# Sixteen 32x32 tiles for the last stage of the kernels' transform, and another memory order for its two results

## The chip, the cores and the metric

The kernel runs on one core of one Trainium2 chip. The metric is the device time of one execution in microseconds (us): the median of three runs, beside the lowest and the highest. The profile is of a further execution, which has its own time and its own span (first to last instruction).

The engines are called as in the profile: PE (TensorE's matmuls) and PEld (its weight loads), DVE (VectorE), ACT (ScalarE), POOL (GpSimd), SP (SyncE, whose queue starts most DMAs). PSUM is the matmuls' result memory, here eight banks of 128 partitions x 512 f32.

## What is computed

Four layers on a sequence of 2048 rows of 640 channels: attention, a state-space layer, attention, the same state-space layer.

```python
x = x + A(layernorm(x))      # attention, 32 heads of 20 channels, projection wo
x = x + B(layernorm(x))      # state-space layer
x = x + A(layernorm(x))
x = x + B(layernorm(x))

# B: a convolution as long as the sequence, one kernel per channel, by FFT
P = exp((A * dt)[:, :, None] * pos)
K = 2.0 * einsum("dn,dnl->dl", C, P).real       # 640 kernels of 2048 values
y = irfft(rfft(u, 4096) * rfft(K, 4096), 4096)[:, :, :2048]
return y + u * D_skip
```

The kernels K are the same in both B layers, so their transform is computed once.

## The kernel before, in words

**The stages in order of time.** First attention, beside which a generator `kgen` computes K and stores it in DRAM (`kd`). Then the first output projection (`out_proj`, lines 1130 to 1150), beside which the kernels' transform (`ktransform`, lines 1056 to 1125) runs. Then the first state-space layer (`ssm`, lines 1165 to 1303). Then attention, output projection and `ssm` once more, without `kgen` and without the transform.

**The output projection** handles 16 row tiles `s`. For each it loads a 128 x 640 piece of the attention's result (`otl`), splits it into two parts (`oh` on ACT, `ol` on DVE), runs 30 matmuls of 128 x 320 into two PSUM tiles of the pool M, adds them to `x`, and after every second `s` makes the normalised rows `uh` and `ul` that `ssm` reads (ACT, then POOL). `ssm` can begin when all sixteen are there.

**The kernels' transform** handles five blocks of 128 channels (`unit_load(b)`):
1. Load 1 MB, `kl` (128 channels x 2048), two buffers, the next block's load started at the block's begin; add the skip value to the first column.
2. 16 transposes in four groups into PSUM tiles `pkt` (pool T, two banks); ACT writes `ktrh`, DVE the remainder `ktrl`, both f16.
3. Eight PSUM tiles `pkx` (pool X, two banks), 12 f16 matmuls each; ACT or DVE copies each into `x1` (profile name `kx`).
4. A loop over eight quarters `q` of 4 x 128 columns: four transposes of `x1` into `pkt` (pool T); ACT scales them into `xt` (`kxt`); one f32 matmul with the 128 x 128 matrix `f2` into `pkf` (pool F, two banks; the profile shows it as two instructions of 128 x 512); two shuffles on DVE, which write the result's real half twice into `kn0` and its imaginary half twice into `kn1`; a multiplication of `kn1` by a sign per partition, on ACT. After two quarters `kn0` and `kn1` (512 KB each) are stored into the DRAM tensors `kha` and `khb`.

**In `ssm`** each of 40 steps loads a quarter of a block of both tensors, `ka` and `kb` (256 KB each, three buffers each), multiplies by `ka` on DVE (`t1`), by `kb` on POOL (line 1226) and adds on POOL (line 1227).

**What sets the order.** Each engine works through its own list in order. The lists are made when the program is built: of the instructions whose inputs and buffers are free by then, the one that the code emitted first goes first. `out_proj` emits the whole transform in the middle of its third row tile (`weave(1000)`), so the transform goes first and the later row tiles fill the time in which it waits. A buffer pool that is opened over the memory of earlier pools waits for the last use of those. During attention most orders are tied by hand (`chain`); in the transform and in `out_proj` none are.

Of the kernel before, what the change touches and what calls it, by code (L numbers as in the profile page):

```python
# [21 lines left out]
P = 128  # L22
L = 2048
# [61 lines left out]
def mha_s4d_kernel(ctx, tc, x_in, wqkv, wo, lar, aim, cr, ci, ldt, dsk,  # L85
                   c_e1, c_eb, c_f2, c_fa, c_sel, c_lv, c_id, c_sg, c_e16, c_f16, c_id16, out, parts="asas", general=None):
# [28 lines left out]
    kha = dram.tile([P, D // 4, P], F32, name="kha")  # L115
    khb = dram.tile([P, D // 4, P], F32, name="khb")
# [933 lines left out]
    DUP0 = list(range(16)) * 2  # L1050
    DUP1 = list(range(16, 32)) * 2

# [3 lines left out]
    def ktransform(e1):  # L1056
# [4 lines left out]
        f2 = c1.tile([P, P], F32, name="f2")  # L1061
        sy.dma_start(f2, c_f2)
        sgn = c1.tile([P, 1], F32, name="sgn")
        sy.dma_start(sgn, c_sg)

        skip = c1.tile([P, NCT], F32, name="skip")
        sy.dma_start(skip, dsk)

        def load(b):
            kl = c2.tile([P, L], F32, name="kl")  # L1070
            sy.dma_start(kl, kd[b * P:b * P + P, :])
            return kl
        kls = [load(0)]

        def unit_load(b):
            kl = kls.pop()
            if b + 1 < NCT:
                kls.append(load(b + 1))
# [11 lines left out]
            x1 = c1.tile([P, 32, NI // 2, 16], F32, name="kx1")  # L1090
            for i2 in range(NI // 2):
                ps = pst("X", [P, 2, 2, P], F32, tag="X", name="pkx")
                for i in range(2):
                    s = 2 * i2 + i
                    for r in range(2):
                        for n, (e, m) in enumerate(((0, hi), (0, lo), (1, hi))):
                            te.matmul(ps[:, r, i, :], e1[:, e, s, r, :], m[:, s, :], start=(n == 0), stop=(n == 2))
                (ve.tensor_copy if i2 % 4 == 1 else se.copy)(by_channel(x1, i2), ps.rearrange("p r i (g c) -> p (r i) g c", c=4))
                yield
            prev = None  # L1100
            for q in range(9):
                if q < 8:
                    pt = pst("T", [P, 4, P], F32, tag="T", name="pkt")
                    for g in range(4):
                        te.transpose(pt[:, g, :], x1[:, 4 * q + g].rearrange("p i s -> p (i s)"), ident)
                    xt = c2.tile([P, 512], F32, name="kxt")
                    se.activation(xt, pt.rearrange("p g k -> p (g k)"), AF.Copy, scale=ksc[:, 1:2])
                if prev is not None:
                    g0 = b * 32 + 4 * (q - 1)
                    if q % 2:  # L1110
                        kn = [c2.tile([P, 2, 512], F32, name=f"kn{s}") for s in range(2)]
                    px = pst("F", [P, 512], F32, tag="F", name="pkf")
                    te.matmul(px, f2, prev, start=True, stop=True)  # L1113
# [49 lines left out]
    def ssm(x, uh, ul, consts, last):  # L1163
# [19 lines left out]
        with ExitStack() as c:  # L1183
# [29 lines left out]
            def stage2b(b, q, xt):  # L1213
# [3 lines left out]
                sy.dma_start(ka, kha[:, g0:g0 + 4, :].rearrange("p g k -> p (g k)"))  # L1217
                sy.dma_start(kb, khb[:, g0:g0 + 4, :].rearrange("p g k -> p (g k)"))
# [217 lines left out]
def _constants():  # L1436
# [13 lines left out]
    for s, o, m in ((0, 0, C), (1, 0, S), (0, 1, -S), (1, 1, C)):  # L1450
        fa[:, s, :, :, o] = np.einsum("hli,cd->hlcid", m.reshape(4, 4, 16), e4)
    f2 = f2.reshape(2, NI // 2, 2, 4, P).transpose(1, 0, 2, 3, 4)
    sg = np.zeros((4, 2, 16, 1))
    sg[:, 0], sg[:, 1] = -1.0, 1.0
# [5 lines left out]
    cs = dict(c_e1=e1.reshape(P, -1), c_eb=eb.reshape(P, -1), c_f2=f2.reshape(P, P), c_sg=sg.reshape(P, 1),  # L1460
              c_fa=fa.reshape(P, -1), c_sel=sel.reshape(P, -1), c_lv=lv, c_id=np.eye(P))
    cs = {n: np.ascontiguousarray(a.astype(np.float32)) for n, a in cs.items()}
    for n, a in (("c_e16", e1), ("c_f16", f2)):
# [9 lines left out]
          "c_e1", "c_eb", "c_f2", "c_fa", "c_sel", "c_lv", "c_id", "c_sg",  # L1473
# [31 lines left out]
```

## Time and profile before

| | us |
|---|---|
| time, median of 3 runs | 2690.48 |
| lowest to highest | 2688.76 to 2694.98 |
| the profiled execution, time | 2693.68 |
| its span | 2691.8 |
| first attention, first S matmul to last row | 113.3 to about 1102 |
| first output projection, its matmuls | 1102.3 to about 1273 |
| transform, first to last matmul | 1132.8 to 1246.9 |
| first `ssm`, first matmul | 1272.9 |

The granted clock of TensorE was 0.996 over the span. A row of a group reads: line, engine, operation, written tile <- read tiles, shape and type, count; then busy time, mean ns of one. Line 77 is the helper through which ACT, DVE, POOL and SP operations of the ordered engines go, so these are told apart by their tiles. A matmul's duration has its way through the array in it: the time from one start to the next is shorter. In rows by stretch the columns are the stretch, its length, the busy time of each engine (with its number of instructions), then the granted clock, the mean busy share of the 16 DMA engines, and GB/s.

### The profile page before, as it was taken

To read this page: it belongs to the slowest core of one execution; us is meant where nothing else is said; L and a number is where in the kernel's file an instruction comes from. 1 tells how busy PE (TensorE), PEld (TensorE's weight loads), DVE (VectorE), ACT (ScalarE), POOL (GpSimd) and SP (SyncE) were. 2 spreads that over 40 slices of the span, in tenths; PEclk is the share of its full clock that TensorE was granted. 3 is DMA by queue.
4 is the path that set the end of the run, shared out by engine and by line. 5 is a ranking of instruction groups with operands and counts; after the bars stand their busy time and mean duration, and the time that the engine had idled before them with its cause. 6 is when DMAs were issued, how large, how long until landed. Compare 5 with 4: busy or idle time off the path is not lost.

```text
span 2691.8 us, 116010 instructions
## 1 busy us (share of the span) xinstructions
PE 2519.0 (94%) x51104; PEld 1432.0 (53%) x51104; DVE 1473.7 (55%) x3295; ACT 2364.3 (88%) x2799; POOL 855.2 (32%) x1283
## 2 busy tenths in 40 slices
PE   7899999999999998899998999999999998888998
PEld 3345444444444443678886444454444443335888
DVE  8687877876856993477776332232232221003865
ACT  7899999999999999676655899999999999996464
POOL 1123323333332334301671122222222223222476
PEclk9999999999999999999999999999999999999999
DMA  6513222322221225354542111111121112112365
GB/s 212 177 49 88 64 77 53 88 58 72 62 54 50 56 66 169 109 229 161 185 146 65 49 52 52 52 56 42 47 63 39 52 39 59 41 37 80 115 189 162
DMA packets 183154, 236.48 MB, mean 88 GB/s; under 512 B 42864, under 2 KB 128368, under 8 KB 180976
## 3 DMA queue, kind: packets, MB, share of 16 engines
q1 hardware_dynamic: 146304, 182.38, 21.2%
q0 software_dynamic: 36336, 46.59, 7.4%
q8 instruction: 403, 6.60, 1.0%
q14 instruction: 111, 0.91, 0.1%
HBM read 152.81 MB, written 76.03 MB: 85 GB/s over the span
## 4 chain that ended last, share of the span: by engine, by line
ACT 50%; PE 27%; issue 9%; DVE 6%; DMA 3%; SPq 1%; POOL 0%; ACTq 0%; DVEq 0%; POOLq 0%
ACT pt L77 49%; PE pa L862 4%; PE psv L1233 3%; PE psy L1243 3%; PE S L845 3%; PE po L1139 2%; PE psx L1221 2%; PE m L598 2%; PE psx L1198 1%; PE po L1133 1%; PE pkf L1113 1%; PE pst L1208 1%; DVE ktab L77 1%; DMA qop<-qs 1%; PE pq L751 1%
## 5 line engine op out<-in xcount | busy, mean ns | idle before, releaser
L77 ACT ACTIVATE pt<-S 128x1024 f32<-128x1024 f32 x2048 | 1921.9, 1037 | 37.5 <-PE S L845 28.4
L862 PE MATMUL pa<-pt,V 64*32 64x512 f32 x16384 | 1102.2, 590 | 1.7 <-DVE oc L77 1.2
L845 PE MATMUL S<-qop,kop 61*32 61x512 f16 x16384 | 883.6, 381 | 114.4 <-ACT pt L77 102.6
L845 PEld LDWEIGHTS <-kop 61*32 61x32 f16 x16384 | 374.0, 89 | 772.3 <-issue 651.4
L862 PEld LDWEIGHTS pa<-pt,V 64*32 64x32 f32 x16384 | 316.9, 106 | 73.4 <-issue 9.1
L77 POOL DMA_DIRECT2D dn<-oc x256 | 126.2, 499 | 709.3 <-DVE oc L77 682.4
L77 DVE TENSOR_SCALAR qc<-m 128x512 f32<-128x512 f32 (+1 forms) x68 | 46.8, 689 | 305.0 <-PE m L598 302.4
L77 DVE COPY oc<-pa 128x512 f32<-128x512 f32 x64 | 44.2, 690 | 305.1 <-PE pa L862 297.4
L77 POOL DMA_DIRECT2D db<-dn x256 | 129.5, 511 | 129.7 <-DMA dn<-dr 126.4
L598 PE MATMUL m<-xh,wh 64*32 64x512 f16 x2560 | 147.9, 379 | 5.0 <-DVE qc L77 5.0
L598 PE MATMUL m<-xh,wl 64*32 64x512 f16 x2560 | 148.7, 377 | 0.0
L598 PE MATMUL m<-xl,wh 64*32 64x512 f16 x2560 | 146.6, 377 | 0.0
L598 PEld LDWEIGHTS <-wh 64*32 64x32 f16 x5120 | 92.8, 93 | 78.0 <-issue 35.7
L77 POOL DMA_DIRECT2D ot<-oc x256 | 130.3, 516 | 3.1 <-DVE oc L77 1.7
L1226 POOL TENSOR_TENSOR t<-t,kb 128x512 f32<-128x512 f32 x80 | 101.9, 1275 | 67.8 <-DVE t L77 66.8
L77 ACT COPY xt<-pst 128x1024 f16<-128x1024 f16 x80 | 81.6, 1023 | 46.7 <-PE pst L1208 46.6
L77 POOL DMA_DIRECT2D dn<-dr x64 | 35.8, 560 | 245.3 <-DVE dr L77 235.5
L77 DVE TENSOR_TENSOR kb<-ktab 128x512 f32<-128x512 f32 x160 | 107.7, 692 | 0.0
L77 DVE TENSOR_SCALAR V<-m 128x160 f32<-128x160 f32 x64 | 20.7, 324 | 157.7 <-PE m L564 157.7
L564 PEld LDWEIGHTS <-xh 128*128 128x128 f16 x960 | 79.7, 98 | 47.0 <-issue 31.6
L1227 POOL TENSOR_TENSOR t<-t,t 128x512 f32<-128x512 f32 x78 | 99.3, 1273 | 8.6 <-DVE t L77 2.6
L320 PEld LDWEIGHTS m<-kb,ka 128*32 128x32 f32 x3840 | 61.0, 109 | 72.0 <-issue 56.1
(281 smaller groups left out, 3970.2 us busy)
## 6 DMA issues: line engine op xcount, KB each, us to landing
ka<-kha SPq DMA_DIRECT2D x80, 256.0 KB
kb<-khb SPq DMA_DIRECT2D x80, 256.0 KB
db<-dn POOLq DMA_DIRECT2D x256, 64.0 KB, 2.5
kpw<-wd POOLq DMA_DIRECT2D x60, 192.0 KB, 5.0
qop<-qs SPq DMA_DIRECT2D x256, 40.0 KB
kop<-ks SPq DMA_DIRECT2D x128, 80.0 KB
ot<-oc POOLq DMA_DIRECT2D x256, 40.0 KB, 2.7
otl<-ot SPq DMA_DIRECT2D x32, 320.0 KB
```

The source lines that it names most:

```text
L77: made = f(out, *a, **k)
L320: chain(te.matmul(ps[32 * j:32 * j + 32, c8, :], a[n][:, ch, :], b[n][:, dd, :], start=(n == 0), stop=(n == 2), tile_position=(0, 32 * j)))
L564: chain(te.matmul(ps[:, :n], a_[:, ct, sl], m[:, ct, :], start=(k == 0), stop=(k == 14)))
L598: chain(te.matmul(ps[r][32 * t:32 * t + 32, :], a_[rows, ct, 32 * u:32 * u + 32], m[rows, ct, 512 * v:512 * v + 512], start=(k == 0), stop ...
L845: chain(te.matmul(S[32 * t:32 * t + 32, 512 * r:512 * r + 512], kt_[rows, kc + 32 * t:kc + 32 * t + 32], qt[rows, :], start=True, stop=Tru ...
L862: chain(te.matmul(pa[r][32 * j:32 * j + 32, :], V[rows, kt, VP * h:VP * h + 32], pts[j // 2][rows, 512 * (j % 2):512 * (j % 2) + 512], sta ...
L1139: te.matmul(pos[hf], oh[:, ct, :], m[:, ct, 320 * hf:320 * hf + 320], start=False, stop=(ct == NCT - 1 and m is wol))
L1221: te.matmul(px, f2[:, f, :], xt[:, k, :], start=(n == 0), stop=(n == 2))
L1226: ge.tensor_mul(t2, t2, kb)
L1227: (ge if g0 else ve).tensor_add(t1, t1, t2)
L1233: te.matmul(pv[:, g].rearrange("p r i c -> p (r i c)"), t1[:, g * P:g * P + P], fa, start=True, stop=True)
L1243: te.matmul(py[:, i, :], eb[:, 4 * i4 + i, r, :], v[:, r, 4 * i4 + i].rearrange("p g c -> p (g c)"), start=(r == 0), stop=(r == 1))
```

## The change

Only the transform and the places that read its results change.

- **Order of channels.** `kl` is loaded with its partitions in the order (c, g) in place of the channels' own order, where channel = 4g + c; `dsk` likewise. `kl` now has one buffer, and the next block's load is emitted after the block's 16 transposes.
- **PSUM.** The pools T and F (two banks each) are gone; `pkt` takes turns with `pkx` in X (two banks), and a new F holds four tiles F0 to F3 of one bank each. M is as before.
- **Last stage.** The block's eight quarters become two halves t. `turned(t)` makes four groups of four transposes and four scalings into one tile `xt` of 128 x 2048 (two buffers). `ends(t, xt, s, dst)` runs sixteen matmuls, each on a 32x32 tile of the array (row group ch, column group g) with a 32 x 32 piece of `f2` and 512 columns, into the four F banks; for s = 0 `f2` gives the real half twice, for s = 1 the imaginary half twice with its sign. Four copies (two DVE, two ACT) bring the banks to `kn`, and two stores of 512 KB follow. The order is: turned(0), ends(0, real), turned(1), ends(0, imaginary), ends(1, real), ends(1, imaginary).
- **Gone**: the shuffles, the sign multiplication, the constant `c_sg`.
- **Memory order.** `kha` and `khb` are [10, 128, 4, 4, 128]. A store still writes 4 KB in a row per partition. `ka` and `kb` are read with four pieces of 512 B for each partition, where it was one of 2 KB.

```diff
-    kha = dram.tile([P, D // 4, P], F32, name="kha")
-    khb = dram.tile([P, D // 4, P], F32, name="khb")
+    kha = dram.tile([2 * NCT, P, 4, 4, P], F32, name="kha")
+    khb = dram.tile([2 * NCT, P, 4, 4, P], F32, name="khb")
...
         def load(b):
-            kl = c2.tile([P, L], F32, name="kl")
-            sy.dma_start(kl, kd[b * P:b * P + P, :])
+            kl = c1.tile([P, L], F32, name="kl")
+            sy.dma_start(kl, kd[b * P:b * P + P, :].rearrange("(g c) l -> c g l", c=4))
...
-                pt = pst("T", [P, 4, P], F32, tag="T", name="pkt")
+                pt = pst("X", [P, 4, P], F32, tag="X", name="pkt")
...
+            if b + 1 < NCT:
+                kls.append(load(b + 1))
+            x1 = c1.tile([P, 4, NI // 2, 4, 32], F32, name="kx1")
...
-            prev = None
-            for q in range(9):
-                if q < 8:
-                    pt = pst("T", [P, 4, P], F32, tag="T", name="pkt")
+
+            def turned(t):
+                xt = c2.tile([P, 4, 4, P], F32, name="kxt")
+                for q in range(4):
+                    pt = pst("X", [P, 4, P], F32, tag="X", name="pkt")
                     for g in range(4):
-                        te.transpose(pt[:, g, :], x1[:, 4 * q + g].rearrange("p i s -> p (i s)"), ident)
-                    xt = c2.tile([P, 512], F32, name="kxt")
-                    se.activation(xt, pt.rearrange("p g k -> p (g k)"), AF.Copy, scale=ksc[:, 1:2])
-                if prev is not None:
-                    g0 = b * 32 + 4 * (q - 1)
-                    if q % 2:
-                        kn = [c2.tile([P, 2, 512], F32, name=f"kn{s}") for s in range(2)]
-                    px = pst("F", [P, 512], F32, tag="F", name="pkf")
-                    te.matmul(px, f2, prev, start=True, stop=True)
-                    for s in range(2):
-                        ve.stream_shuffle(kn[s][:, (q - 1) % 2, :], px, [DUP0, DUP1][s])
-                    se.activation(kn[1][:, (q - 1) % 2, :], kn[1][:, (q - 1) % 2, :], AF.Copy, scale=sgn)
-                    if q % 2 == 0:
-                        for s, dst in enumerate((kha, khb)):
-                            sy.dma_start(dst[:, g0 - 4:g0 + 4, :].rearrange("p g k -> p (g k)"),
-                                         kn[s].rearrange("p q k -> p (q k)"))
-                prev = xt
+                        te.transpose(pt[:, g, :], x1[:, :, :, :, 16 * t + 4 * q + g].rearrange("p c i s -> p (c i s)"), ident)
+                    se.activation(xt[:, q], pt, AF.Copy, scale=ksc[:, 1:2])
+                return xt
+
+            def ends(t, xt, s, dst):
+                px = [pst("F", [P, 512], F32, tag=f"F{ch}", name=f"pkf{ch}") for ch in range(4)]
+                for ch in range(4):
+                    rows = slice(32 * ch, 32 * ch + 32)
+                    for g in range(4):
+                        te.matmul(px[ch][32 * g:32 * g + 32, :].rearrange("p (q k) -> p q k", k=P), f2[rows, s, :],
+                                  xt[rows, :, g, :], start=True, stop=True, tile_position=(32 * ch, 32 * g))
+                for h in range(2):
+                    kn = c2.tile([P, 2, 4, P], F32, name=f"kn{s}")
+                    for ch in range(2):
+                        (se.copy if ch else ve.tensor_copy)(kn[:, ch], px[2 * h + ch].rearrange("p (q k) -> p q k", k=P))
+                    sy.dma_start(dst[2 * b + t][:, 2 * h:2 * h + 2], kn)
+            xts = [turned(0)]
+            for t in range(2):
                 yield
+                ends(t, xts[t], 0, kha)
+                yield
+                if t == 0:
+                    xts.append(turned(1))
+                yield
+                ends(t, xts[t], 1, khb)
+            yield
...
-                sy.dma_start(ka, kha[:, g0:g0 + 4, :].rearrange("p g k -> p (g k)"))
-                sy.dma_start(kb, khb[:, g0:g0 + 4, :].rearrange("p g k -> p (g k)"))
+                for t, src in ((ka, kha), (kb, khb)):
+                    sy.dma_start(t.rearrange("p (g k) -> p g k", k=P),
+                                 src[g0 // 16].rearrange("(g a) c q k -> (a c) g q k", g=4)[:, :, q % 4])
...
-                    psum(c3, M=2, T=2, F=2)
+                    psum(c3, M=2, F=1)
```

More of the change, by code (lines that the diff above doesn't have):

```diff
@@ L1060, in ktransform @@
         c2 = c.enter_context(tc.tile_pool(name="f2", bufs=2))
[L1061 to L1064, printed above, removed]
+        f2 = c1.tile([P, 2, 32], F32, name="f2")
+        sy.dma_start(f2, c_f2.rearrange("p (s m) -> p s m", s=2))
         skip = c1.tile([P, NCT], F32, name="skip")
-        sy.dma_start(skip, dsk)
+        sy.dma_start(skip, dsk.rearrange("(g c) n -> c g n", c=4))
         def load(b):
-            kl = c2.tile([P, L], F32, name="kl")
-            sy.dma_start(kl, kd[b * P:b * P + P, :])
+            kl = c1.tile([P, L], F32, name="kl")
+            sy.dma_start(kl, kd[b * P:b * P + P, :].rearrange("(g c) l -> c g l", c=4))
             return kl
@@ L1451, in _constants @@
         fa[:, s, :, :, o] = np.einsum("hli,cd->hlcid", m.reshape(4, 4, 16), e4)
+    k2 = f2[:, :, 0, :, :, :, 0]
+    k2 = np.stack([k2[:, :, :, [0, 0]], k2[:, :, :, [1, 1]] * np.array([-1.0, 1.0])[:, None]], axis=2)
+    k2 = k2.reshape(2, NI // 2, 2, 2, 32).transpose(1, 0, 2, 3, 4).reshape(1, 32, 64)
+    k2 = np.repeat(k2, 4, axis=0)
     f2 = f2.reshape(2, NI // 2, 2, 4, P).transpose(1, 0, 2, 3, 4)
-    sg = np.zeros((4, 2, 16, 1))
-    sg[:, 0], sg[:, 1] = -1.0, 1.0
     sel = np.zeros((P, NBLK, H))
```

14 lines of the change are left out of this document (5 added, 9 removed).

## The prediction

> **What bounds the kernel now.** I read the page first, for the span and the engines' shares, and then went to the only place that the change touches much: the transform beside the first output projection.
>
> ```profile
> span 2691.8 us, 116010 instructions
> PE 2519.0 (94%) x51104; PEld 1432.0 (53%) x51104; DVE 1473.7 (55%) x3295; ACT 2364.3 (88%) x2799; POOL 855.2 (32%) x1283
> ```
>
> The shares are averages over stages. Busy time by stretch, first of everything, then of the matmuls into `po` alone (columns: PE, PEld, DVE, ACT, and in the first fence POOL):
>
> ```profile
> 1132.00:1252.00 120.00, 118.34 (x960) 91.39 (x959) 91.84 (x249) 92.87 (x151) 9.17 (x7) 1.00 0.56 215
> 1252.00:1274.00 22.00, 22.00 (x161) 21.41 (x160) 15.97 (x46) 8.55 (x14) 6.16 (x4) 1.00 0.16 53
> ```
>
> ```profile
> 1132.00:1252.00 120.00, 32.85 (x160) 23.80 (x159) 5.26 (x11) 1.00 0.56 215
> 1252.00:1274.00 22.00, 21.07 (x141) 20.32 (x139) 4.34 (x9) 1.00 0.16 53
> ```
>
> While the transform runs PE is busy for 118.3 of 120 us, DVE and ACT for 92 and 93: PE is the bound, because the output projection's matmuls fill its waits (160 of them, 32.9 us). The 141 that found no hole run afterwards, 21.1 us with PE at 100%, and only then does `ssm` begin:
>
> ```profile
> L1198 PE MATMUL psx<-uh,e1s x640: 216/219/230, 1272.9 to 2645.9; 128*128 128x128 f16 x160
> ```
>
> So PE time saved in the transform is worth its full amount, as long as the 141 matmuls move forward into it. The most to be had is that tail, 21 us.
>
> What the last stage costs, groups of the stretch 1132 to 1252:
>
> ```profile
> L77 DVE STREAM_SHUFFLE kn<-pkf 128x512 f32<-128x512 f32 x80 | 54.2, 736 | 0.0
> ...
> L77 ACT ACTIVATE kn<-kn,sgn 128x512 f32<-128x512 f32 x40 | 28.4, 722 | 1.5 <-DVE kn L77 0.9 <-DVE va L77 0.2
> ...
> L77 ACT ACTIVATE kxt<-pkt,ksc 128x512 f32<-128x512 f32 x40 | 26.5, 676 | 8.8 <-PE pkt L1105 8.8
> ...
> L77 ACT COPY kx<-pkx 128x512 f32<-128x512 f32 x30 | 17.4, 583 | 6.4 <-PE pkx L1097 6.3
> ...
> L77 DVE COPY kx<-pkx 128x512 f32<-128x512 f32 x10 | 6.8, 685 | 3.2 <-PE pkx L1097 3.2
> ```
>
> and PE's list over one quarter of a block:
>
> ```profile
> 1192.68 0.60 PE L1105 MATMUL pkt<-ident,kx 128*128 128x128 f32 x4
> 1193.12 1.02 PE L1113 MATMUL pkf<-kxt,f 128*128 128x512 f32 x2
> 1193.97 0.60 PE L1105 MATMUL pkt<-ident,kx 128*128 128x128 f32 x4
> ```
>
> Four transposes take 0.44 us from start to start, the f32 matmul 0.85 (its 1.02 holds the way out of the array), a quarter 1.29.
>
> **The change, part by part.** *The matmuls.* Removed: 5 blocks x 8 = 40 of 0.85 us, 34.0 us of PE. Added: 5 x 4 = 20 groups of sixteen tiles. The nearest row is attention's `pa`: eight tiles of 64 x 32, f32, 512 columns, sixteen instructions, and the next matmuls behind them:
>
> ```profile
> 1096.03 1.05 PE L862 MATMUL pa<-pt,V 64*32 64x512 f32 x16
> 1096.89 0.41 PE L845 MATMUL S<-qop,kop 61*32 61x512 f16 x8
> ```
>
> 0.86 us from start to start: eight tiles take what one full matmul takes. Sixteen are not in this trace. If all run at once a group is 0.86 us; if only eight do, 1.72. I take 0.86, because the eight already fill the whole array and sixteen of half the height fill it too. The Trainium skill ("TensorE: Matmul & The Clock Gate", Part 3 on packing small matmuls) gives 10.6 times for sixteen 32x32 tiles with 512 columns, so nearly all at once; by it the group would be some 0.06 us longer.
>
> The array also changes its tile shape before and after each group. What that costs stands where attention goes from `S` (64x32 tiles) to full matmuls and back:
>
> ```profile
> 618.17 0.58 PE L845 MATMUL S<-qop,kop 61*32 61x512 f16 x8
> 618.68 0.24 PE L564 MATMUL m<-vh,xh 128*128 128x160 f16 x1
> ...
> 619.10 0.23 PE L564 MATMUL m<-vh,xh 128*128 128x160 f16 x1
> 619.17 0.23 PE L564 MATMUL m<-vl,xh 128*128 128x160 f16 x1
> 619.34 0.41 PE L845 MATMUL S<-qop,kop 61*32 61x512 f16 x8
> ```
>
> The step back to `S` is 0.17 us where equal neighbours are 0.07 apart: 0.10 us a change of shape, 0.20 a group. So 20 x (0.86 + 0.20) = 21.2 us, and the term is 21.2 - 34.0 = -12.8 us; with eight at a time 20 x 1.92 = 38.4, +4.4.
>
> *The copies.* DVE loses 80 shuffles (54.2 us) and gains 40 copies of 0.685 (27.4); ACT loses 28.4 and gains 40 of 0.583 (23.3). Both have room beside PE, so I count nothing; less DVE work (27 us) frees the banks sooner. Nothing at all stays free only while PE is the bound: the rivals below price the other case.
>
> *The first load of `kl`.* Before, `kl` had memory of its own and was loaded during attention; the tiles of its neighbour pool, `f`, `sgn` and `skip`, came only when attention's memory was given back:
>
> ```profile
> 1048.94 0.33 SPq L77 DMA_DIRECT2D kl<-kd  x1
> ...
> 1128.95 0.35 SPq L77 DMA_DIRECT2D f<-in_c_f  x1
> ...
> 1130.38 0.43 SPq L77 DMA_DIRECT2D skip<-in_dsk  x1
> ```
>
> ```profile
> 1132.27 0.51 DVE L77 TENSOR_TENSOR kl<-kl,skip 128x1 f32<-128x1 f32 x2 [0.45 <-DMA skip<-in_dsk]
> ```
>
> Now `kl` is in that pool, so I expect its load at about 1130, queued on SP behind the others, and the transform starts later than 1132.3 by the load. How long is 1 MB? DMA shares and rates in four stretches (the last two columns): the load of `kl` at 1050; a load of `qop`, whose source has a first dimension of 2; a load of `otl`, 512 B pieces; and `ssm`, 2 KB pieces.
>
> ```profile
> 1050.00:1053.00 3.00, 2.31 (x64) 0.91 (x55) 0.00 (x0) 3.00 (x5) 0.60 (x1) 1.00 0.83 303
> 1055.70:1056.10 0.40, 0.40 (x16) 0.16 (x8) 0.00 (x0) 0.40 (x1) 0.00 (x0) 1.00 0.14 49
> ...
> 1254.00:1256.00 2.00, 2.00 (x15) 1.89 (x14) 1.48 (x4) 0.73 (x1) 0.00 (x0) 1.00 0.55 164
> 1291.00:1303.00 12.00, 11.46 (x126) 9.98 (x127) 10.03 (x22) 8.50 (x16) 10.45 (x9) 1.00 0.64 200
> ```
>
> Over all engines 1.05 MB at 303/0.83 = 365 GB/s is 2.9 us. But the `qop` load kept 0.14 of the 16 engines busy, two of them, as many as its source's first dimension; the new source of `kl` has a first dimension of 4. On four engines the load would be 2.9 x 4 = 11.5 us. The Trainium skill ("DMA: Bandwidth & Descriptors", on why a DMA increments its semaphore by 16) says that a DMA runs on the largest number up to 16 that divides the slowest dimension of both sides; by it four, and the `qop` row agrees. So the transform starts between 1 and 10 us late. PE has the output projection to do meanwhile, if the order was made so; unhidden 0 to 10, I take 3, since row tiles come before the transform already now. The other four loads are emitted after the block's transposes and have the rest of a block, some (1252 - 1132)/5 = 24 less 5 us, against 11.5: hidden. On SP such a load waits for the last of those transposes, and `otl` loads and `kn` stores issued behind it wait with it; the stores come half a block later and `otl` is two row tiles ahead, so I price that at 0, at most the 11.5 us of one load once.
>
> *Loads in `ssm`.* 512 B pieces moved at 164/0.55 = 298 GB/s of full share, the present ones at 200/0.64 = 313: the share goes from 0.64 to 0.67. A step of `ssm` is set by POOL,
>
> ```profile
> L1226 POOL TENSOR_TENSOR t<-t,kb x80: 1258/1276/1286, 1288.4 to 2673.5; 128x512 f32<-128x512 f32 x80
> L1227 POOL TENSOR_TENSOR t<-t,t x78: 1266/1272/1282, 1292.2 to 2674.8; 128x512 f32<-128x512 f32 x78
> ```
>
> 1.276 + 1.272 = 2.55 us, and 512 KB at 298 GB/s take 1.76. Three buffers hide it; zero. If that cover went, each of 80 steps would pay the excess over 2.55.
>
> *Sum.* -12.8 + 3 = -9.8 us: 2693.7 to 2683.9 for the profiled execution, and from the median 2690.5 to 2680.7. The profiled execution is 3.2 us over the median, which lies inside the runs shown (2688.8 to 2695.0), so the difference is carried over as it is.
>
> **The rivals.** *The chain sets the end, no change.* With PE relieved, the transform's own chain may be last. Its quarters took 8 x 1.29 = 10.3 us a block. Now: `turned(0)`, four scalings of 0.676, 2.7 us; then four times a group (1.06) and two copies in a row on each of ACT and DVE (2 x 0.685), 2.43, as each F bank exists once: 9.7. Together 12.4, 2.1 more a block, 10.5 in all, and up to 9 for the late start. The transform, with its copies done at about 1249, would end at 1268.5, and `ssm` would begin 4 us earlier: 2686. For it: ACT at 93 of 120 us loses only 5. Against it: the next block's transposes and first stage, 24 - 10 = 14 us, need X and not F and can run beside the groups. Chance 0.22.
>
> *PE stands empty at the F banks, slower.* The same banks, seen from PE: after each group the next waits for two copies and the way out of the array (1.02 - 0.85), 1.37 + 0.17 = 1.54 us. `turned(1)` (4 x 0.44 = 1.76) covers one of a block's four gaps; 15 are left, and `pkt` has lost its own two banks, so less can be put there. All 15 empty cost 23 us: -9.8 + 23 = +13, 2704. It decides from 9.8/1.54, over 6 empty gaps of 15. For it: the list is fixed before anything is timed. Against it: now PE lacks 1.7 us in 120. Chance 0.15. The Trainium skill ("TensorEngine Tiling (Array Packing)", PSUM Bottleneck) warns of just this, that tiling speeds up PE and leaves the emptying of PSUM as the bound; by this row of PE it isn't so yet.
>
> *Only eight tiles at once*: +4.4 + 3 = +7, 2698; slower, chance 0.05. *The 512 B loads bind in `ssm`*: it takes under 524 KB/2.55 us = 206 GB/s where `otl` had 298; at 190 the step is 2.76 and 80 steps cost 17 us, 2698 with the gain. Chance 0.03. *It doesn't do what it says*: PE saves its 12.8 us, but all 10 us of the late load stand on PE: -3, 2688. Chance 0.02.
>
> **How the numbers follow.** The forecast has 0.53; its own range is from 2668 (the whole tail, -21, and a little of the 1.7 us in which PE is idle) to 2685. The range of 8 in 10 goes on through the chain case and the late load (0.24 together) and ends at 2700, which takes in the eight-tile case and the milder end of the empty banks. About 0.2% (5.4 us) is what a measurement of this kernel can tell from no change: faster, under 2685.1, 0.53; same 0.24; slower 0.15 + 0.05 + 0.03 = 0.23.
>
> **What would show it.** Right: sixteen-tile groups (32 instructions) start to start near 1.06 us; PE over 95% busy through the transform; under 60 `po` matmuls after the last group; `ssm` begins near 1263; DVE's busy time 27 us lower. Wrong: `kl` loaded before 1100, or its landing under 5 us after its issue (the four-engine reading); PE waiting for copies out of `pkf` for more than 10 us in all; POOL in `ssm` waiting for `kb`; or the first `psx` of `ssm` later than 1273.

## The result, and the profile after

| | before | after |
|---|---|---|
| time, median (runs) | 2691.77 us (4) | 2781.23 us (4) |
| lowest to highest | 2688.76 to 2694.98 | 2779.88 to 2788.68 |
| ratio, 95% interval | | 1.0337, 1.0318 to 1.0356 |
| first matmul of the first `ssm` | 1272.9 us | 1366.8 us |

The change makes the kernel slower by 3.4%, some 90 us, where 10 us less were forecast. A fourth run of before moved its median from 2690.48 to 2691.77. The profiled execution of after took 2788.68 us, the longest of its four runs. Its first page rows:

```profile
span 2786.9 us, 117028 instructions
...
PE 2535.2 (91%) x51664; PEld 1441.6 (52%) x51664; DVE 1444.8 (52%) x3175; ACT 2361.9 (85%) x2799; POOL 852.6 (31%) x1283
```

DVE has 29 us less to do (1473.7 before), as reckoned, and it helps nobody. The first matmul of `ssm`, of the groups by tile:

```profile
L1202 PE MATMUL psx<-uh,e1s x640: 216/219/229, 1366.8 to 2741.0; 128*128 128x128 f16 x160
```

It starts at 1366.8 in place of 1272.9, 93.9 us later; the span grew by 95.1. So nearly the whole loss lies ahead of it, beside the transform. After's busy time by stretch (columns as before: PE, PEld, DVE, ACT, POOL, granted clock, DMA share, GB/s):

```profile
1132.00:1153.00 21.00, 4.72 (x31) 4.20 (x29) 4.24 (x12) 1.45 (x3) 2.71 (x2) 0.72 0.39 81
1153.00:1200.00 47.00, 34.16 (x359) 27.87 (x360) 17.97 (x35) 22.57 (x37) 3.35 (x2) 0.80 0.37 121
1200.00:1250.00 50.00, 31.14 (x385) 24.25 (x384) 14.96 (x32) 21.83 (x37) 2.79 (x2) 0.86 0.39 129
1250.00:1300.00 50.00, 28.11 (x302) 20.04 (x302) 13.68 (x28) 19.22 (x32) 2.80 (x2) 0.74 0.35 122
1300.00:1350.00 50.00, 43.31 (x492) 29.25 (x492) 21.33 (x41) 29.64 (x50) 2.79 (x2) 0.84 0.43 165
```

PE, busy for 118 of 120 us before, stands empty for 77 of these 218; so do DVE and ACT. Nothing is the bound here; everybody waits. The clock, 1.00 before, is granted at 0.72 to 0.86. For whom they wait, from the waits of the stretch 1130 to 1360:

```profile
DVE kl L77 <- DMA kl<-kd: 76.5, 5, 16.2
ACT kx L77 <- PE pkx L1091: 67.9, 22, 14.5
...
PE pkx L1091 <- DVE kx L77: 50.1, 4, 13.5
DVE kn L77 <- PE pkf L1110: 31.1, 17, 5.5
...
PE pkt L1077 <- DVE lt L77: 16.4, 1, 16.4
```

DVE waits five times, once a block, for the load of `kl`, 76.5 us in all; PE waits 50.1 us for DVE's copies of `pkx`, and ACT 67.9 us for PE. PE's wait of 16.4 us is that of the first block: its transposes start right behind the first addition to `kl` on DVE (`lt` is DVE's next operation). DVE's list shows how one becomes the other:

```profile
1201.15 0.67 DVE L77 COPY kx<-pkx 128x512 f32<-128x512 f32 x1
...
1202.52 0.16 DVE L77 SCALAR_TENSOR_TENSOR nb<-mv,rs 128x2 f32<-128x2 f32 x1
1218.06 0.16 DVE L77 TENSOR_TENSOR kl<-kl,skip 128x1 f32<-128x1 f32 x1 [15.38 <-DMA kl<-kd]
1218.14 0.68 DVE L77 COPY kx<-pkx 128x512 f32<-128x512 f32 x1
```

A block has two `kx` copies on DVE. Between them the list has the addition of the skip value to the *next* block's `kl`. It waits 15.4 us for its load, and the copy behind it, which needs nothing of that load, waits too; PE then finds X full. The same in the chain of waits (start, length):

```profile
1132.06 20.79 DMA kl<-kd
...
1159.07 18.14 DMA kl<-kd
...
1198.21 19.83 DMA kl<-kd
...
1239.37 19.08 DMA kl<-kd
...
1283.82 17.84 DMA kl<-kd
```

Each load takes 18 to 21 us; the three of before that were issued beside the transform landed 4.5 to 5.9 us after their issue. Three stretches in the middle of such loads, with all engines empty (the last three columns are the clock, the DMA share and GB/s):

```profile
1212.00:1216.00 4.00, 0.00 (x0) 0.00 (x0) 0.00 (x0) 0.00 (x0) 0.00 (x0) 0.50 0.25 80
1248.00:1252.00 4.00, 0.00 (x0) 0.00 (x0) 0.00 (x0) 0.00 (x0) 0.00 (x0) 0.81 0.24 61
1252.00:1256.00 4.00, 0.00 (x0) 0.00 (x0) 0.00 (x0) 0.00 (x0) 0.00 (x0) 0.50 0.25 76
```

The share is 0.24 to 0.25, four of the sixteen DMA engines, at 61 to 80 GB/s. The last stage itself, in PE's list:

```profile
1184.82 1.14 PE L1110 MATMUL pkf<-kxt,f 32*32 32x512 f32 x32
1185.89 1.16 PE L1101 MATMUL pkt<-ident,kx 128*128 128x128 f32 x8
1186.98 1.04 PE L1110 MATMUL pkf<-kxt,f 32*32 32x512 f32 x2
1187.95 0.71 PE L1101 MATMUL pkt<-ident,kx 128*128 128x128 f32 x4
...
1192.46 1.69 PE L1110 MATMUL pkf<-kxt,f 32*32 32x512 f32 x32 [0.32 <-DVE kn L77]
1194.08 1.17 PE L1077 MATMUL pkt<-ident,kl 128*128 128x128 f32 x8
```

A group of sixteen tiles (32 instructions) whose banks are free takes 1.07 us to the next start; where the banks come free one after another it takes 1.62.

In `ssm` nothing changed: POOL's multiplication by `kb` lasts as long as before (1.276), so the loads in pieces of 512 B stay hidden.

```profile
L1231 POOL TENSOR_TENSOR t<-t,kb x80: 1263/1273/1287, 1382.7 to 2768.5; 128x512 f32<-128x512 f32 x80
```

### The profile page after: what moved, and what is told of

It is laid out like the page before. It is cut to its first block, busy times and chain, and to the rows that moved or that the text cites. A ratio compares the mean times of both kernels' runs of the same rounds, so it can differ in the third digit from the quotient of the medians.

```text
span 2786.9 us, 117028 instructions
## 1 busy us (share of the span) xinstructions
PE 2535.2 (91%) x51664; PEld 1441.6 (52%) x51664; DVE 1444.8 (52%) x3175; ACT 2361.9 (85%) x2799; POOL 852.6 (31%) x1283
## 4 chain that ended last, share of the span: by engine, by line
ACT 50%; PE 25%; issue 9%; DVE 6%; DMA 5%; POOL 0%; SPq 0%; ACTq 0%; DVEq 0%; POOLq 0%
ACT pt L77 49%; PE pa L862 4%; DMA kl<-kd 3%; PE psv L1238 3%; PE po L1143 2%; PE psy L1248 2%; PE S L845 2%; PE psx L1226 2%; PE m L598 1%; PE psx L1202 1%; PE po L1137 1%; PE pst L1212 1%; PE pq L751 1%; PE pkf L1110 1%; DVE ktab L77 1%
## 5 line engine op out<-in xcount | busy, mean ns | idle before, releaser
L77 ACT ACTIVATE pt<-S 128x1024 f32<-128x1024 f32 x2048 | 1922.4, 1037 | 40.4 <-PE S L845 30.9
L1047 POOL TENSOR_TENSOR ul<-u,uh 128x640 f16<-128x640 f32 x30 | 46.9, 1579 | 257.3 <-ACT uh L77 257.3
```

What stands on the lines that cost most here:

```text
L77: made = f(out, *a, **k)
L1047: (ve if s == NI - 1 else ge).tensor_sub(ul[:, s, :], u, uh[:, s, :])
```

## The experiments

After the result two theories stood against each other. By the first, the load of `kl` is dear because of its arrangement: it is issued late, into one buffer, and asked for in the middle of DVE's list; a block ahead it would be hidden. By the second, a load on four DMA engines is so slow that it costs wherever it stands. Beside both it was open what the F banks and the shared X lose under cover of that wait. Each time below is a median; the ratio is against runs of the kernel before on the same chip, whose median was 2693.45 to 2693.78 us in every set.

| run | us | ratio, 95% interval |
|---|---|---|
| e1: after, load of `kl` in four DMAs | 2712.71 | 1.0064, 1.0047 to 1.0082 |
| e3: before, with after's load | 2744.47 | 1.0186, 1.0163 to 1.0208 |
| e5: after, addition on POOL | 2740.27 | 1.0159, 1.0137 to 1.0181 |
| e6: e1, `kl` in memory of its own | 2713.51 | 1.0061, 1.0040 to 1.0082 |
| e7: before, X shared | 2697.15 | 1.001, 1.000 to 1.002 |
| e8: e1, copies not from the banks | 2701.26 | 1.003, 1.002 to 1.004 |
| e9: e1, interleaved | 2709.47 | 1.0051, 1.0033 to 1.0068 |
| e10: e1, groups whole | 2713.25 | 1.0067, 1.0051 to 1.0084 |
| e11: e9 + e6 + e10 | 2700.43 | 1.0027, 1.0017 to 1.0038 |
| e12: e11, emission spread | 2695.73 | 1.0008, 0.9997 to 1.0018 |
| e13: e11, spread from row tile 3 | 2699.83 | 1.0026, 1.0014 to 1.0037 |
| e14: e12, `kxt` on two engines | 2695.70 | 1.0005, 0.9996 to 1.0014 |
| e15: before, emission spread | 2695.27 | 1.0005, 0.9996 to 1.0014 |
| e16: e12, groups twice | 2705.93 | 1.0045, 1.0031 to 1.0059 |
| e17: e15, matmuls twice | 2724.41 | 1.0114, 1.0099 to 1.013 |

**The load, e1 and e3.** e1 moves the same bytes to the same places in four transfers, one per row group:

```diff
-            sy.dma_start(kl, kd[b * P:b * P + P, :].rearrange("(g c) l -> c g l", c=4))
+            src = kd[b * P:b * P + P, :].rearrange("(g c) l -> c g l", c=4)
+            for c_ in range(4):
+                sy.dma_start(kl[32 * c_:32 * c_ + 32, :], src[c_])
```

> The changed kernel, but each 1 MB load of kl is four loads of 32 channels, so that the first dimension of each is 32 and not 4. Theory A: the change is slow because a load of kl with a first dimension of 4 runs on four DMA engines and takes 18 to 21 us in place of about 5, and DVE waits for it in its list (76.5 us in all) with the copies of kx behind it. Then the four loads together land within 7 us of their issue, DVE waits less than 15 us for kl, and the time is 2670 to 2705 us. Theory B: the groups of sixteen tiles, with one buffer for each F bank and X shared, are slow by themselves: 2740 us or more. Theory C: it is the one buffer and the load emitted late, whatever it runs on: the wait for kl stays over 40 us and the time over 2740.

e3 puts after's single load into the kernel before, with its two buffers:

```diff
-            sy.dma_start(kl, kd[b * P:b * P + P, :])
+            sy.dma_start(kl, kd[b * P:b * P + P, :].rearrange("(g c) l -> c g l", c=4))
```

> The kernel before, with kl loaded in the order (c, g) of the changed kernel, first dimension 4; its two buffers and the load a block ahead are kept. The channels then stand in another order than the rest expects, so the numbers of the result are not the reference's; the work is the same. Theory A: the load takes 18 to 21 us here too, but it has a whole block of about 24 us: 2690 to 2705 us, DVE's wait for kl under 15 us. Theory E, the load on four engines holds up everything behind it in the same DMA rings (stores of kha and khb, otl): over 2715 us.

e1 gets 68.5 of the 90 us back, and no wait for `kl`'s load is left in it. Its loads land 6 to 7 us after the first issue; its time is still 8 us above theory A's range, while B and C, at 2740 us or more, are out. But e1 changes more than the load. The list that was made for it has the addition elsewhere: behind both `kx` copies, among the copies into `kn`, and DVE reaches it 13 to 17 us after the issue (in after 3 to 5):

```profile
1173.52 1.71 SPq L77 DMA_DIRECT2D kl<-kd  x4
...
1186.28 0.69 DVE L77 COPY kn<-pkf 128x512 f32<-128x512 f32 x1 [3.59 <-PE pkf L1112]
1186.89 0.15 DVE L77 TENSOR_TENSOR kl<-kl,skip 128x1 f32<-128x1 f32 x1
```

So e1 can't tell the speed of the load from the place of its user. The kernel before and e3 can, for both have the addition ahead of the second `kx` copy, as after has, and DVE reaches it 3 to 5 us after the issue in both. This is before, whose waits for such loads beside the transform are 3.3 us in all:

```profile
1141.49 0.16 DVE L77 TENSOR_TENSOR kl<-kl,skip 128x1 f32<-128x1 f32 x1 [1.82 <-DMA kl<-kd]
1142.06 0.69 DVE L77 COPY kx<-pkx 128x512 f32<-128x512 f32 x1 [0.42 <-PE pkx L1097]
```

e3 is 51 us slower than before, where the theory of the arrangement (A in its text) had it nearly unchanged. Its waits for the load, and its loads after the first two:

```profile
DVE kl L77 <- DMA kl<-kd: 46.4, 3, 16.6
```

```profile
L77 SPq DMA_DIRECT2D kl<-kd x3: 527/527/561, 1144.7 to 1223.2; - x3
```

So the form of the load is enough by itself, without tiles, banks or a new order. The time lies in theory E's range, but E's mechanism does not show: no engine waits for `otl`, `kha` or `khb` there. And the trace says why the second buffer is no help: the load issued at 1144.7 is asked for by DVE at 1147.8 already (its wait of 16.6 us ends at 1164.4). The load was emitted a block ahead, but the list puts its user right behind it. Both theories have a part, and the next run changes the place alone.

**The list, e5.** The addition goes to POOL, which has little else to do here; the load stays on four engines.

```diff
-            ve.tensor_add(kl[:, 0:1], kl[:, 0:1], skip[:, b:b + 1])
+            ge.tensor_add(kl[:, 0:1], kl[:, 0:1], skip[:, b:b + 1])
```

> The changed kernel, its slow load kept, but the addition of the skip value to kl's first column moves from DVE to POOL. Theory A with the list as its second half: kl's wait no longer holds the copies of kx on DVE and with them PE; four of the five waits (60 us) have the rest of a block beside them, only the first one (21 us, nothing to do before it) stays: 2715 to 2740 us. If the length of the load is all and the list plays no part (theory D): the next block cannot start before its kl, the time stays at 2770 to 2785.

```profile
POOL kl L1071 <- DMA kl<-kd: 119.8, 5, 31.4
...
PE pkt L1077 <- POOL kl L1071: 15.4, 1, 15.4
ACT kx L77 <- PE pkx L1091: 15.1, 21, 1.2
```

POOL now waits 119.8 us, longer than DVE did (a part of it before the load is even issued; the loads still land 17.5 to 20 us after their issue), and the time falls by 41 us, to the upper end of what was expected: behind POOL's wait stands almost nobody (15.4 us of PE in the first block), and ACT's waits for `pkx` go from 67.9 to 15.1. So with this slow load 41 of the 90 us come from the place of one small addition in a list.

**What is left of e1: 19 us over before, and 10 us of gain missing.** PE's list in e1 shows the same picture as after's at the groups, now without the load:

```profile
1188.93 1.13 PE L1112 MATMUL pkf<-kxt,f 32*32 32x512 f32 x30
1190.88 1.59 PE L1112 MATMUL pkf<-kxt,f 32*32 32x512 f32 x32 [0.81 <-ACT kn L77]
1192.80 1.69 PE L1112 MATMUL pkf<-kxt,f 32*32 32x512 f32 x32 [0.32 <-DVE kn L77]
1194.42 1.17 PE L1079 MATMUL pkt<-ident,kl 128*128 128x128 f32 x8
```

Three groups stand in a row, with `po` matmuls left over for the end, and each waits for the copies of the one before. That is theory F (each F bank exists once); against it stood X (the shared pool X). A third candidate shows in e1's waits: `kn` has two buffers for each half, and a copy into it also waits until an earlier store has landed:

```profile
ACT kn L77 <- DMA khb<-kn: 4.4, 6, 1.9
...
DVE kn L77 <- DMA khb<-kn: 4.1, 6, 1.8
```

Four such stores, 15.5 us together, stand on the chain of work that ended last in e1's transform. No run gives `kn` more buffers, so what they cost is open.

*e6*, the late first load: `kl` gets a pool of its own, and its first load starts at 1051.8, not 1128.3.

```diff
+        ck = c.enter_context(tc.tile_pool(name="fk", bufs=1))
...
-            kl = c1.tile([P, L], F32, name="kl")
+            kl = ck.tile([P, L], F32, name="kl")
```

> As the four loads, and kl (still one buffer) in a pool of its own that does not lie over attention's last memory, so that block 0 can be loaded during attention as it was before. Theory A, with what the prediction said of the first load: the first load is issued before 1100 us and costs nothing, 3 to 10 us less than the four loads alone, 2665 to 2695 us. If the four loads alone leave no wait for the first block, the two are equal within 3 us.

The transform's first transposes then start at 1136.0 in place of 1142.2, and the time does not change: by itself the late load costs nothing that can be measured, presumably since the blocks wait later anyway.

*e7* is one part of the change in the kernel before (both kinds of `pkt` take their banks from X), *e8* takes the banks' readers away from e1:

```diff
-                pt = pst("T", [P, 4, P], F32, tag="T", name="pkt")
+                pt = pst("X", [P, 4, P], F32, tag="X", name="pkt")
...
-                    psum(c3, M=2, T=2, F=2)
+                    psum(c3, M=2, F=2)
```

> The kernel before, with one part of the change alone: the transposes of both kinds (pkt) take their PSUM tiles from pool X, which pkx uses, and pool T is gone. The run with four loads per block was 19 us slower than before although nothing waited for kl any more, and two parts of the change are left for that. Theory X (the shared banks): pkt waits for the banks that ACT and DVE still read, as it did there (9 us on pkt's matmuls and their weight loads behind ktrl), so 10 us or more here too: over 2700, with PE waits for ktrl or kxt of over 6 us. Theory F (each F bank exists once, so the next group waits for the copies of the one before): the F banks are here as before, two of them, so no more than 4 us: 2690 to 2698.

```diff
-                        (se.copy if ch else ve.tensor_copy)(kn[:, ch], px[2 * h + ch].rearrange("p (q k) -> p q k", k=P))
+                        (se.copy if ch else ve.tensor_copy)(kn[:, ch], xt[:, 2 * h + ch])
```

> The run with four loads per block, with the copies into kn reading from SBUF (the group's input kxt, same shape and number, same engines) instead of from the four F banks. So nothing reads the banks and no group waits for one; the results stored are the inputs of the last stage, not its outputs. Theory F: the 24 us of waits of PE and its weight loads for kn go, and a group takes 1.07 us always: 15 to 22 us under the run with four loads, 2690 to 2698. Theory X: the groups' waits are covered and the transposes' waits for X stay: within 6 us of the run with four loads, 2706 to 2714.

Sharing X costs 3.5 us in the kernel before (ratio 1.001, 1.000 to 1.002); what it costs in after was not measured apart. The F banks cost 11.4 us (2712.7 to 2701.3), which lies between the two theories' ranges and under the 15 to 22 expected. e8's three groups in a row, where the clock was 1.00:

```profile
1165.36 3.70 PE L1112 MATMUL pkf<-kxt,f 32*32 32x512 f32 x94
1168.99 1.17 PE L1079 MATMUL pkt<-ident,kl 128*128 128x128 f32 x8
```

They take 3.63 us, 1.21 each and not the 1.07 expected; e1's three took 5.49 (1188.93 to 1194.42). That is 1.86 us a block, some 9 of the 11.4 us. In e8 other waits grow, those of PE's weight loads for `kxt` from 6.1 to 9.1 us.

*e9* emits the next block's transposes of `kl` in two halves between a block's last groups; *e10* ties the second group behind the transposes of `turned(1)`, so that no tile of it stands alone (in the fence of after the pair at 1186.98, 0.97 us to the next start); *e11* is e9, e10 and e6 together.

```diff
+            hl = next(nxt) if nxt else None
+            for s, dst in enumerate((kha, khb)):
+                for _ in range(2):
+                    if nxt:
+                        next(nxt)
+                    yield
+                ends(1, xts[1], s, dst)
```

> The run with four loads per block, with the next block's transposes of kl emitted in two halves between the last groups of a block instead of behind them, so that PE has eight transposes (about 1 us) to do while the copies empty the F banks. Theory F: the gaps ahead of the third and fourth group of a block (0.8 and 0.3 us, and 0.5 and 0.6 us of a group that runs bank by bank) go: 5 to 12 us under the run with four loads, 2700 to 2708. Theory X: the transposes now ask for X at the time that DVE copies kn, so they wait for ktrl instead, and nothing is won: 2708 to 2716.

```diff
-                        te.matmul(px[ch][32 * g:32 * g + 32, :].rearrange("p (q k) -> p q k", k=P), f2[rows, s, :],
+                        made = te.matmul(px[ch][32 * g:32 * g + 32, :].rearrange("p (q k) -> p q k", k=P), f2[rows, s, :],
...
+                        if after is not None:
+                            tie(made, after.ins)
```

> The run with four loads per block, with one thing in PE's list changed: in it one tile of the second group of each block stands alone between the transposes of turned(1) (a pair of instructions, 0.97 us from its start to the next), and the other fifteen behind them; here the group is tied behind the last transpose. Theory S (a tile that runs alone costs what sixteen cost): 5 x 0.97 = 4.8 us less, 2706 to 2710. Rival: PE waits at that place for the scaled kxt and for a bank of X anyway, so nothing changes: 2711 to 2715.

> Three edits on the run with four loads per block: the next block's transposes between the last groups, kl in a pool of its own (first load during attention), and the second group of a block whole. Theory F (once PE no longer waits at the F banks, the late first load shows): 8 to 14 us under the run with four loads, 2699 to 2705. Rival (what is won at one place is lost at the next, since nothing but the transform's own chain stands between the groups): 2706 to 2713.

e9 alone won 3 us, which decides nothing, and e10 none, as its rival had it: the lone tile would then have stood where PE waited in any case. Together with the early load they win 12.3 us, as theory F had it. In e9 the transform starts at 1145.4, in e11 at 1132.5; so the late load seems to show once the waits at the banks are covered, though no run joins e9 and e6 without e10.

*e12* and *e13* give PE something to do between the groups, as `out_proj` now emits the transform in small pieces; *e15* does this in the kernel before, as a control.

```diff
-                if s == 2:
-                    weave(1000)
+                if s >= 0:
+                    weave(3 if s < NI - 1 else 1000)
```

> The kernel with those three edits, with the transform emitted in pieces of three steps over all row tiles of the output projection, not all of it in the third row tile; in the last three blocks 8 to 20 matmuls into po then stand between the groups and between the pkx tiles. Theory F (PE stands at the F and X banks because its list has nothing else at that place, though po matmuls are left over for the end): 5 to 15 us under the kernel with the three edits, 2686 to 2698. Rival (the transform's own chain of copies is the bound): the same within 4 us or slower, since the transform ends later.

> As the kernel before it, with the pieces spread from the third row tile on, so that po matmuls stand between the groups of more blocks and only some 10 are left behind the last group. Theory F: within 4 us of the kernel before it or up to 6 under it, 2682 to 2700. Rival: the transform ends last and holds up the state-space layer: 5 to 20 us over the kernel before it.

> The kernel before, with nothing but the transform emitted in pieces of four steps over all row tiles of the output projection, as control of the spread. Theory: PE was 98 percent busy there (167.3 of 170.6 us up to the first psx), so the spread has at most 3 us to win: 2690 to 2695, the same within 0.1 percent. Rival (spreading is worth something by itself): 2686 or less, and then what the spread kernel won over the changed one says nothing of the change.

e12 is 4.7 us faster than e11 by the medians and equal to the kernel before; e13 loses that again (its transform ends at about 1275, and `ssm` starts 3.2 us later than in e12). e15 changes nothing: what e12 won is not the spread's own. So with the load and the order mended, sixteen tiles give a kernel that is neither faster nor slower. No version was faster than the kernel before.

**Where the 12.8 us of the groups went.** Busy time from the first `po` matmul to the first `psx`: before, then e1, then e12.

```profile
1102.30:1272.90 170.60, 167.34 (x1286) 138.66 (x1280) 127.47 (x346) 113.07 (x181) 29.58 (x32) 1.00 0.50 185
```

```profile
1100.10:1291.40 191.30, 174.36 (x1846) 138.56 (x1840) 103.21 (x224) 109.70 (x181) 29.38 (x32) 0.96 0.55 176
```

```profile
1101.50:1272.90 171.40, 161.84 (x1847) 132.32 (x1842) 103.74 (x228) 108.92 (x181) 29.63 (x32) 0.99 0.58 190
```

In e12 PE is busy for 5.5 us less than before and idle for 6.3 more (9.6 against 3.3), so the stretch is as long. In e1 PE is even busy longer, by 7.0, though it computes less: the clock is 0.96, and a group that runs bank by bank counts as busy. e14 tried the chain through X, with half of the `kxt` on DVE:

```diff
+                    if q % 2:
+                        ve.tensor_scalar_mul(xt[:, q], pt, ksc[:, 1:2])
+                    else:
```

> The spread kernel, with every second kxt (the scaled copy of the transposes) on DVE, the others on ACT as before, so that a block's eight come out of pool X twice as fast. Up to the first psx the spread kernel has PE busy for 5.5 us less than the kernel before (161.8 against 167.3) and idle for 6.3 us more (9.6 against 3.3), so it ends equal. Theory C (the 16-tile groups do save PE time, and the chain of copies through X holds it back: PE and its weight loads wait 3.6 and 5.8 us for kxt): 3 to 7 us under the spread kernel, 2688 to 2693. Rival (PE's idle time moves to the next wait, kx or kn or ktrl): within 2 us of the spread kernel.

Nothing changed, as the rival had it. The last two runs price a group and a matmul by doubling each:

```diff
-                for ch in range(4):
+                for _ in range(2):
+                    for ch in range(4):
```

> The spread kernel, each group of sixteen tiles issued twice into the same banks (the second time over the first result). Prices a group without a new copy or bank: 20 more groups. Theory P (PE time decides there and sixteen tiles run at once): each adds 0.86 us and no change of shape, 17 us, 2709 to 2716. If PE's idle 9.6 us swallow part: 8 to 16 us. If only eight run at once: 34 us.

```diff
-                    te.matmul(px, f2, prev, start=True, stop=True)
+                    for _ in range(2):
+                        te.matmul(px, f2, prev, start=True, stop=True)
```

> The kernel before with the spread emission, each f32 matmul into pkf issued twice into the same bank: 40 more matmuls of 0.85 us, which is what the change removes. Theory P: PE is full, so 34 us, 2727 to 2732; the difference to the run with groups twice, 40 x 0.85 - 20 x 0.86 = 17 us, is then what the groups themselves save. Rival (a matmul is hidden in a wait that PE has anyway): under 25 us.

The matmuls into `pkf` alone, busy time over the same stretch of e15, e17, e12 and e16:

```profile
1100.50:1271.00 170.50, 41.62 (x80) 1.00 0.52 185
```

```profile
1101.70:1305.30 203.60, 75.13 (x160) 1.00 0.43 155
```

```profile
1101.50:1272.90 171.40, 25.96 (x640) 0.99 0.58 190
```

```profile
1105.30:1293.80 188.50, 47.45 (x1280) 1.00 0.52 174
```

Forty more matmuls add 33.5 us to PE, 0.84 each, and 29.1 to the median, between theory P and its rival. Twenty more groups add 21.5 us, 1.07 each; of this 17.1 show in the length of the profiled stretch (171.4 to 188.5), so part of it fell into PE's idle time. The median rises by 10.2 alone, for the profiled execution was the longest of e16's five (2711.54 us). A pair of groups takes

```profile
1152.57 2.35 PE L1117 MATMUL pkf<-kxt,f 32*32 32x512 f32 x64
1154.84 1.16 PE L1107 MATMUL pkt<-ident,kx 128*128 128x128 f32 x8
```

2.27 us to the next start, so the second takes 1.20 (2.27 - 1.07) with no change of shape, as in e8's row of three. (The average of 1.07 is lower because some groups of e12, which it is taken against, run bank by bank: 25.96/20 = 1.30.) At 1.20 a group the change saves PE 33.5 - 20 x 1.20 = 9.5 us rather than 12.8.

The same can be counted in e12 itself, each matmul from its start to the next one's start, or to its own end if that is earlier. Over the stretches above this gives

| us of PE | before | e1 | e12 |
|---|---|---|---|
| into `pkf` | 35.2 | 32.9 | 24.9 |
| transposes into `pkt` | 26.5 | 31.8 | 30.9 |
| into `pkx` | 26.8 | 28.1 | 27.5 |
| into `po` | 78.9 | 81.5 | 78.6 |

So the groups save 10.3 us in e12, and the transposes that now stand between them take 4.4 more. The last transpose ahead of a group takes 0.205 us to the group's start, where its like ahead of a full matmul takes 0.11: that is the 0.10 us of a change of shape that was forecast, but only a part of the 4.4. What is left, 5.5 us, e12's longer idle time (6.3) uses up.

## Why the prediction was wrong

**The step that failed** is "The other four loads are emitted after the block's transposes and have the rest of a block, some (1252 - 1132)/5 = 24 less 5 us, against 11.5: hidden", with SP's wait priced "at 0, at most the 11.5 us of one load once". Two things in it were wrong.

- *The load was mis-sized.* Four engines were right: the share is 0.25, and the Trainium skill's rule ("DMA: Bandwidth & Descriptors", why a DMA increments its semaphore by 16) stands. But 2.9 x 4 = 11.5 us takes for granted that each of the four moves what each of sixteen does, 365/16 = 23 GB/s. In the stretches shown they moved 61 to 80 GB/s together, 15 to 20 each, and a load took 18 to 21 us.
- *The deadline was mis-placed.* I gave the load until the end of the block, where its data are used. The list puts the first user, a 0.16 us addition, in the middle of the block, 3 to 5 us after the issue, ahead of work that doesn't need it. Even a load of 11.5 us would have been waited for there, an estimate of 7 to 8 us a block. "At most one load once" was five loads, 76.5 us of waits.

It took both. e5 shows that with this load the place alone is worth 41 us; before and e3, which share the place, show 3.3 us of waits with a fast load and 46.4 with this one. The place could have been seen: DVE's wait of 1.82 us at 1141.49 stands in the trace of before.

**The bound.** "PE time saved in the transform is worth its full amount" holds only as long as PE is full. PE was idle for 77 of 218 us in after, and even in e12 for 9.6.

**The matmuls.** A group at 1.07 to the next start, where its banks were free, against the 1.06 predicted, looks like a hit, but it was made of 0.86 and two changes of shape, and e8 and e16 have groups at 1.20 without any change of shape. In e12 the groups took 24.9 us of PE and the transposes beside them 4.4 more than before, 29.3 in all, where the sum had 21.2 with the changes of shape: the term is about -6, not -12.8. That sixteen tiles run at once was right, since eight at a time would have made it 1.7. The Trainium skill ("TensorE: Matmul & The Clock Gate", Part 3) has the time of such a pack as one matmul and some 4 ns for each further tile, an estimate of 0.84 + 0.06 = 0.90 us here; no group of these runs was that short, and the measurement decides.

**The copies** cost what was said (0.69 and 0.59 us each) and were priced at nothing "while PE is the bound". They were the next to show: the rival "PE stands empty at the F banks" was right in its mechanism. It gave 1.54 us for each of 15 gaps, 23 us; e8 prices it at 11.4, since three groups in a row lose 1.86 us a block and not three times 1.54. It is what the Trainium skill warns of ("TensorEngine Tiling (Array Packing)", PSUM Bottleneck), and here the runs agree with it. The price of `pkt` in X, which I had left inside this rival, is 3.5 us by e7, in the kernel before.

**The first load** was priced at 3 of 0 to 10 us, and this too failed in after: the first transposes start at 1153.2 in place of 1132.8, and PE is busy for 4.7 of the 21 us from 1132. Once the load is fast, its late start costs nothing in e6 by itself. In e11, where it is early, the gain over e9 is 9.0 us, though the groups are kept whole there as well.

**The loads in `ssm`**: hidden, as said.

Of the signs that I named, the landing under 5 us stayed out, as four engines should have it. Two that speak against the sum showed in after: PE waits 5.7 us for copies out of `pkf` and its weight loads 19.9, and `ssm` begins later than 1273. What I missed was asking who stands behind the instruction that waits; I asked it for SP's queue and not for DVE's.

**What stays open.** Why the transposes between the groups take 4.4 us more (some 1.6 of e12's PE time may be the clock, 0.99 over 162 us), and which wait would have to go for the idle 6.3 us to turn into time: e14 only rules out the place that I tried, and the stores of `kn` were not tried. Which of e9's and e10's edits makes e11's gain was not taken apart either, nor why the list came out otherwise for four loads than for one.

## What to carry to other kernels

Before a transfer is called hidden, look up where its first consumer stands in its engine's list and what is queued behind that, not where its data are needed; a small instruction that waits holds up everything behind it. A rearranged source can put a load on a quarter of the DMA engines: look at the first dimension of both sides, and split the load by it, which costs three more issues and no memory. Look at the lists again after such an edit, for they can come out otherwise. And time saved on the bounding engine counts only while the engine that frees its buffers keeps up: give PE other work between groups that fill every bank of a pool.

## What the runs showed of the hardware that was not expected

- Four DMA engines moved 61 to 80 GB/s where the whole set moved 365: 0.17 to 0.22 of it, not 0.25. A load of 1 MB took 18 to 21 us, and 6 to 7 in e1 as four loads over all engines.
- One tile of 32x32 alone (the pair of instructions at 1186.98) took PE 0.97 us to the next start, nearly as long as all sixteen.
- When PE waits, it also slows down: the granted clock was 0.50 while all engines waited for a load, 0.72 to 0.86 over the stretches around, and 0.96 in e1 over 191 us, where it was 1.00 before. In after it stayed at 0.50 for some 4 us when PE had work again at 1218.9:

```profile
1219.00:1222.00 3.00, 3.00 (x19) 3.00 (x18) 0.71 (x2) 1.31 (x2) 0.00 (x0) 0.50 0.00 0
```

The `pkx` matmuls at its begin start 0.107 us apart, in before 0.056. A stall thus costs more than its length.
